# A chunked delta-rule attention with a gated convolution: the dense part taken over pairs of chunks, one merge step over 128 rows, and the order of all instructions written anew

## The chip, the cores and the metric

The kernel runs on one core of a Trainium2 chip. The metric is the device time of one execution in microseconds (us). Engines are named as in the profile: PE multiplies matrices (PEld is its weight load), DVE and ACT are the two vector engines, POOL is the general one, SP issues transfers. All numbers are float32, and the profile counts two matrix instructions for each float32 matmul of the source.

## The reference

Each of 4 x 8 heads has 768 tokens of 48 features. A state of 48 x 48 is updated token by token with the delta rule; the result, heads side by side, goes through a causal convolution of five taps whose sigmoid gates a dense product, and then through a second dense product.

```python
def _attn_ref(q, k, v, beta):
    k_n = k / (norm(k, axis=-1) + 1e-06)
    for t in range(S):
        y[:, :, t] = einsum('bhd,bhde->bhe', q[:, :, t], state)
        v_old = einsum('bhde,bhd->bhe', state, kt)
        state = state + bt[:, :, :, None] * einsum('bhd,bhe->bhde', kt, vt - v_old)

def _moe_ref(x, w_val, conv_w, w_out):      # x: (4, 768, 384)
    for k in range(5):
        gate_pre += conv_w[k] * xp[:, k:k + S, :]
    return (1 / (1 + exp(-gate_pre))) * (x @ w_val) @ w_out
```

## The kernel before, in words

The 768 tokens are cut into 12 chunks of 64 (`C`, `NCH`); two chunks are a pair `g`. In each chunk the 32 heads lie as 16 units in each half of the 128 partitions. Per chunk there are four kinds of work.

**Products of keys and queries.** `kq` multiplies keys with keys and queries on PE; ACT copies the key product to `GL` (`kqevac`), DVE writes the query product times a causal mask (`masked`, called by `att` and `att0`): for head half h = 0 in two operations of 64 rows straight into `R`, for h = 1 in one of 128 rows into `AQ`, which two transfers then bring into `R` (`stack`).

**The triangular inverse.** The state equation needs the inverse of a 64 x 64 triangular matrix per head. Per pair, DVE transposes blocks of `GL` into `TL` (`trans_in`, L463), inverts 16 x 16 blocks there in a long chain of small operations (`coef`, `row`, `mergez8`, `merget8`), and transposes the result out into `XA` and `WB` (`trans_out`, L520). Per chunk, PE and ACT then merge 16 x 16 blocks to 32 (`m16`, `m32`) and 32 to 64 (`lev` twice, with `zevac` and `tevac`), which fills `XX`. In `m16` the weights are `G64` or, in `m32`, `W64`; each matmul uses 64 rows and 64 columns of the array, at four places in turn.

**The recurrence.** `e` (state times keys), `eadd` on DVE, `u` (`XX` times values), `uevac`, `s` (new state into the PSUM tiles `SPS`), `sevac`, and `y` (the chunk's output). `y` needs `Y`, of which one part comes from `US` over a transfer that ACT issues. The chunk's output goes to `X`, 32 of its rows over six transfers of SP from `YSB` (X<-YSB in the rows).

**The dense part**, `moe(ch)`, once per chunk on tiles of 128 features x 256 columns (4 batches x 64 tokens): a scaled copy on ACT (`conv`), twelve multiply-adds on DVE (`tap`, L678), sigmoid on ACT, nine matmuls `val` (L687), three products on DVE (`gate`, L691), six matmuls `outp` (L695), two copies out and four stores.

The order is not a scheduler's: every call is added to a `Plan`, and the tables `ORDER` (numbers of planned calls) and `BANKS` (the PSUM bank for each result) say in which order they are issued. Each engine and each queue takes its own calls in that order. A -1 in `ORDER` is a matmul of zeros (`keep_warm`, L925); there are 31. Loads of chunks 0 to 3 go over SP, later ones over POOL. At the start, the weights, which arrive as 64-bit floats, are turned into float32 by DVE, ACT and POOL (`plan_weights`).

Of the kernel before, what the change touches and what calls it, by code (L numbers as in the profile page):

```python
# [1014 lines left out]
```

## Time and profile before

| | us |
|---|---|
| time, median of 3 runs | 331.96 (329.41 to 334.33) |
| profiled execution, span from first to last instruction | 324.6 |
| PE busy | 280.4 |
| DVE busy | 241.1 |
| ACT busy | 172.1 |
| POOL busy | 77.7 |

The profiled execution's own time is given as its span alone; the median of the runs stands 7.4 above it. Busy times overlap between engines. PE's busy time counts a matmul from its start to its modelled end, so a busy PE may still run at the lower clock: PEclk is the granted TensorE clock as a share of full speed. The mean granted clock of this execution was 0.879.

### The profile page before, as it was taken

What the parts mean: (1) busy time and instruction counts of PE and PEld (TensorE: products, weight loads), DVE (VectorE), ACT (ScalarE), POOL (GpSimd) and SP (SyncE); (2) the same over time, 40 slices, a digit from 0 to 9 for tenths busy, and PEclk for the clock granted to TensorE, in tenths of its full rate; (3) what the DMA queues carried; (4) which work ended last, traced back from release to release, by engine and by line L of the source; (5) the groups of instructions that cost most, each with busy time, mean ns of one, the idle gap of its engine ahead of it and who ended that gap; (6) DMA issues with size and microseconds to landing.
All of it is one profiled execution on the core that took longest, in us unless ns stands there. A gap on an engine that the chain in (4) does not pass through costs nothing.

```text
span 324.6 us, 16708 instructions
## 1 busy us (share of the span) xinstructions
PE 280.4 (86%) x7342; PEld 223.6 (69%) x7342; DVE 241.1 (74%) x602; ACT 172.1 (53%) x454; POOL 77.7 (24%) x156
## 2 busy tenths in 40 slices
...
GB/s 197 217 264 102 256 103 128 82 112 147 131 139 140 177 85 212 61 100 141 137 127 220 30 61 149 193 142 63 34 77 159 95 78 21 6 42 48 79 58 52
DMA packets 50569, 37.84 MB, mean 117 GB/s; under 512 B 37184, under 2 KB 43456, under 8 KB 50496
## 3 DMA queue, kind: packets, MB, share of 16 engines
...
## 4 chain that ended last, share of the span: by engine, by line
PE 49%; DVE 20%; DMA 11%; issue 7%; SPq 4%; ACT 4%; POOL 3%; ACTq 1%; POOLq 0%; DVEq 0%
PE PB L250 24%; PE PB L687 12%; PE PB L695 10%; SPq L237 4%; DMA X<-YSB 4%; DVE GT L678 3%; DMA XX<-in_w_val_dram 3%; DVE KQ L415 2%; PE SPS L250 2%; DMA KQ<-in_qr_dram 2%; DVE PR L489 2%; DMA Y<-US 1%; DVE AQ L415 1%; POOL MASK L276 1%; DVE GL L398 1%
## 5 line engine op out<-in xcount | busy, mean ns | idle before, releaser
L678 DVE SCALAR_TENSOR_TENSOR GT<-X,CW,GT 128x256 f32<-128x256 f32 x144 | 67.9, 497 | 19.4 <-ACT GT L229 17.3
L687 PE MATMUL PB<-X,WV 128*128 128x256 f32 x216 | 59.9, 419 | 2.2 <-issue 2.0
L695 PE MATMUL PB<-WO,GT 128*128 128x384 f32 x144 | 53.3, 511 | 0.7 <-DVE GT L691 0.6
L229 ACT ACTIVATE XX<-PB 32x256 f32<-32x256 f32 (+2 forms) x96 | 39.3, 427 | 19.5 <-PE PB L250 14.1
L687 PEld LDWEIGHTS PB<-X,WV 128*128 128x128 f32 x216 | 41.9, 205 | 10.9 <-issue 3.1
L250 PE MATMUL PB<-KQ 48*64 48x128 f32 (+1 forms) x896 | 36.2, 313 | 15.1 <-DVE QUOT L442 4.0
L250 PEld LDWEIGHTS PB<-KQ 48*64 48x64 f32 x896 | 30.7, 170 | 20.3 <-issue 6.8
L695 PEld LDWEIGHTS PB<-WO,GT 128*128 128x128 f32 x144 | 26.7, 195 | 16.6 <-issue 1.2
L691 DVE TENSOR_TENSOR GT<-PB,GT 128x256 f32<-128x256 f32 x36 | 14.8, 418 | 21.1 <-ACT GT L682 11.4
L250 PE MATMUL PB<-KQ,Y 112*48 112x64 f32 (+2 forms) x768 | 26.5, 227 | 3.3 <-DMA Y<-US 3.3
L229 ACT ACTIVATE GL<-PB 128x256 f32<-128x256 f32 (+1 forms) x44 | 16.3, 403 | 24.7 <-PE PB L250 20.3
L250 PEld LDWEIGHTS PB<-KQ,Y 112*48 112x48 f32 (+2 forms) x768 | 23.8, 128 | 6.4 <-DMA Y<-US 3.8
L582 POOL TENSOR_TENSOR VT<-VT,NRM 128x768 f32<-128x768 f32 x12 | 18.1, 1512 | 40.4 <-DVE NRM L459 19.1
L229 ACT ACTIVATE GT<-X,CW 128x256 f32<-128x256 f32 x36 | 17.8, 504 | 18.3 <-DMA X<-YSB 16.7
L229 ACT ACTIVATE Y<-SPS 48x384 f32<-48x384 f32 (+1 forms) x44 | 20.8, 482 | 7.6 <-PE SPS L250 7.0
L415 DVE TENSOR_TENSOR KQ<-PB,MASK 64x256 f32<-64x256 f32 (+1 forms) x44 | 19.3, 444 | 6.9 <-ACT GT L682 3.1
L250 PE MATMUL PB<-XA,G 64*64 64x16 f32 x768 | 18.0, 222 | 6.7 <-issue 2.9
L250 PEld LDWEIGHTS PB<-XA,G 64*64 64x64 f32 x768 | 16.4, 156 | 9.4 <-issue 3.8
L634 DVE TENSOR_TENSOR VT<-PB,VT 128x384 f32<-128x384 f32 x22 | 11.8, 549 | 12.6 <-PE PB L250 11.7
L250 PE MATMUL PB<-YS,W 64*64 64x32 f32 x768 | 17.5, 237 | 3.5 <-DVE GT L691 1.3
L229 ACT ACTIVATE Y<-PB 64x192 f32<-64x192 f32 x48 | 14.4, 321 | 11.1 <-PE PB L250 7.0
L682 ACT ACTIVATE GT<-GT 128x256 f32<-128x256 f32 x36 | 14.8, 416 | 9.8 <-DVE GT L678 9.5
...
## 6 DMA issues: line engine op xcount, KB each, us to landing
...
```

Of the source, the lines that this page charges most:

```text
L229: A.activation(out=out, in_=in_, func=AF.Copy, **kw)
L237: SP.dma_start(out=dst, in_=src)
L250: PE.matmul(p, lhsT, rhs, start=start, stop=stop, tile_position=(row, col), skip_group_check=True)
L415: V.tensor_tensor(out=AQ[ch % NAQ][:, u:u + n] if v is None else R[ch % NR][r, v, u:u + n], in0=p[r], in1=MASK[h][r].unsqueeze(1).to_broad ...
L489: V.tensor_tensor(out=pr, in0=t8[:, :, 0:i, 0:i], op=ALU.mult, in1=l8[:, :, i, 0:i].unsqueeze(2).to_broadcast([128, 4, i, i]))
L582: G.tensor_tensor(out=v, in0=v, in1=n.unsqueeze(3).to_broadcast([128, 2, HB, D]), op=ALU.mult)
L634: V.tensor_tensor(out=v, in0=bank["e", ch, h][:, 0:HB * D], in1=v, op=ALU.add)
L678: V.scalar_tensor_tensor(out=g, in0=XB[ch % NX][:, m, :, k:k + C], scalar=CW[:, m, k:k + 1], in1=g, op0=ALU.mult, op1=ALU.add)
L682: A.activation(out=g, in_=g, func=AF.Sigmoid, scale=-1.0)
L687: PE.matmul(p[:, 0:B * C], WV[:, k, 128 * m:128 * m + 128], XB[ch % NX][:, k, :, 4:], start=k == 0, stop=k == NKT - 1)
L691: V.tensor_tensor(out=g, in0=bank["val", ch, m][:, 0:B * C].rearrange("p (b t) -> p b t", t=C), in1=g, op=ALU.mult)
L695: PE.matmul(bank["out", ch, i][:, 0:DM], GT[ch % 2][:, k, 2 * i:2 * i + 2, :].rearrange("p b t -> p (b t)"), WO[:, k, :], start=k == 0, st ...
```

## The change

- **Dense part by pairs.** `moe(p, lo, n)` handles 128 tokens of a pair at once: tiles of 128 features x 512 columns. The last two chunks are still done one by one. `X` holds a pair and has two buffers, `GT` five slots.
- **16 to 32 over 128 rows.** `m16` and `m32` contract over all 128 rows: both 64-row halves lie block by block in `XAB` (two copies per pair from `XA`, on POOL, for pair 0 on ACT) and `YS`. There are half as many matmuls, each into one of two column halves of the array, with 32 and 64 columns moved in place of 16 and 32.
- **Masked products.** Both head halves are written to `AQ` by DVE in operations of 128 rows, and four transfers per chunk bring them into `R`, in place of three DVE operations and two transfers.
- **Loads in halves without padding.** Keys, queries and values are loaded by head halves, without the padding rows of before: 48 or 128 rows of 8 units each. The 16 rows of `R` that were padding are filled by POOL at the start (`zR`). `KT`, `VT` and `XX` each have one buffer less.
- `US` goes to `Y` over SP, not ACT. `tevac` is one copy where it was two, and `vscale` is two where it was one. `keep_warm` is called nowhere.
- **Order and banks** are new tables.

```diff
-    NKF, NR, NKTB, NVT, NAQ, NX, NXX, NOS = 4, 4, 3, 3, 2, 3, 4, 3
+    NKF, NR, NKTB, NVT, NAQ, NX, NXX, NOS, NGT = 4, 4, 2, 2, 2, 2, 3, 3, 5
...
-    def masked(p, ch, h, u, n, v):
-
-        r = slice(0, 128) if v is None else slice(64 * v, 64 * v + 64)
-        V.tensor_tensor(out=AQ[ch % NAQ][:, u:u + n] if v is None else R[ch % NR][r, v, u:u + n], in0=p[r],
-                        in1=MASK[h][r].unsqueeze(1).to_broadcast([128 if v is None else 64, n, C]), op=ALU.mult)
+    def masked(p, ch, h, u, n):
+        V.tensor_tensor(out=AQ[ch % NAQ][:, HB * h + u:HB * h + u + n], in0=p, in1=MASK[h].unsqueeze(1).to_broadcast([128, n, C]), op=ALU.mult)
...
+    def xblocks(g, a):
+        r = slice(64 * a, 64 * a + 64)
+        copy(G if g else A, XAB[r, :, 16 * a:16 * a + 16], XA[r])
...
     def l_m16(ch, h):
-        p = bank["m16", ch, h]
-        for pp in range(HB * h, HB * h + HB):
-            for r in (0, 64):
-                to = 64 - r if h else r
-                yield p[to:to + 64, 16 * (pp % HB):16 * (pp % HB) + 16], G64[r:r + 64, unit(ch, pp), :], XA[r:r + 64, unit(ch, pp), :], r, to
+        p = bank["m16", ch]
+        for j in range(HB):
+            x = unit(ch, HB * h + j)
+            yield p[64 * h:64 * h + 64, 32 * j:32 * j + 32], G64[:, x, :], XAB[:, x, :], 0, 64 * h
...
         if what == "U":
-            send(Y[ch % 2][to, v].rearrange("p (h y j) d -> p h y (j d)", h=2, y=2)[:, :, 1], US[ch % 2][other])
-        if what == "A":
-            load(R[ch % NR][to, v, HB:], AQ[ch % NAQ][other])
+            load(Y[ch % 2][to, v].rearrange("p (h y j) d -> p h y (j d)", h=2, y=2)[:, :, 1], US[ch % 2][other])
+        if what != "U":
+            u = slice(HB * what, HB * what + HB)
+            load(R[ch % NR][to, v, u], AQ[ch % NAQ][other if what else to, u])
...
-    def tap(ch, m, k):
-        g = GT[ch % 2][:, m]
-        V.scalar_tensor_tensor(out=g, in0=XB[ch % NX][:, m, :, k:k + C], scalar=CW[:, m, k:k + 1], in1=g, op0=ALU.mult, op1=ALU.add)
...
+    def tap(p, lo, n, m, k):
+        g = gcols(p, m, lo, n)
+        V.scalar_tensor_tensor(out=g, in0=XB[p % NX][:, m, :, lo + k:lo + k + n], scalar=CW[:, m, k:k + 1], in1=g, op0=ALU.mult, op1=ALU.add)
...
+    for i in range(NR):
+        add("POOL", fill, (G, (R[i][32:64, 1], 0.0)), w=[("Rz", i)], kind="zR")
...
     def load_k(ch):
-        fetch(KF[ch % NKF][0:112], kf[ch], ch, [("KF", ch % NKF)], "LKF")
+        for h in range(2):
+            for f in (0, 64):
+                fetch(KF[ch % NKF][f:f + D, HB * h:HB * h + HB], kf[ch, f // 64, :, HB * h:HB * h + HB], ch, [("KF", ch % NKF, h, f)], "LKF")
...
         chain(ch)
-        moe(ch)
+        if ch >= NCH - 2:
+            moe(ch // 2, C * (ch % 2), C)
+        elif ch % 2:
+            moe(ch // 2, 0, 2 * C)
```

Three places of the order follow. The first is DVE at the first inverse (pair 0), from its last reductions to the transposes that end it. Before (PR and TT hold the inverse, TLP is the next pair's input, OS and XX hold raw weights):

```order
L517 TENSOR_REDUCE TT__84<-PR_86 128x2x8x4
L463 STREAM_TRANSPOSE TLP<-GL_73 128x1024
L517 TENSOR_REDUCE TT__84<-PR_85 128x2x8x4
L415 TENSOR_TENSOR KQ<-PB_125,MASK_113 64x512
L520 STREAM_TRANSPOSE WB<-TT__84 128x16x32
L415 TENSOR_TENSOR KQ<-PB_125,MASK_113 64x512
L308 TENSOR_SCALAR XX_79<-XX_79 128x384
L520 STREAM_TRANSPOSE XA<-TT__84 128x16x32
```

And of the change, the same place up to the next pair's input:

```order
L508 TENSOR_REDUCE TT__81<-PR_82 128x2x8x4
L511 STREAM_TRANSPOSE XA<-TT__81 128x16x32
L511 STREAM_TRANSPOSE WB<-TT__81 128x16x32
L405 TENSOR_TENSOR AQ_66<-PB_117,MASK_108 128x256
...
L405 TENSOR_TENSOR AQ_67<-PB_118,MASK_108 128x256
L300 TENSOR_SCALAR OS<-OS 128x384
...
L452 STREAM_TRANSPOSE TLP<-GL_71 128x1024
```

The transpose that opens the second inverse stood ahead of the end of the first; it now stands behind it, behind eight masked products and two sets of weight work.

The second place is POOL ahead of the merge of chunks 8 and 9: W is what `m32` takes as weights, XAB what `m16` moves. Before:

```order
L240 DMA VT_66<-in_vt_dram 128x768
L240 DMA KT_63<-in_kt_dram 128x768
L671 COPY X_92<-X_91 128x12x4
L231 COPY W_75<-WB 32x16x16
L240 DMA KQ<-in_qr_dram 64x1024
L240 DMA KQ<-in_qr_dram 48x1024
L231 COPY W_75<-WB 32x16x16 x3
```

Of the change, ahead of the merge of chunks 6 and 7, the like place:

```order
L232 DMA KQ<-in_kf_dram 48x512
L232 DMA VT_64<-in_vt_dram 128x384
L232 DMA KQ<-in_qr_dram 48x512
L232 DMA KQ<-in_kf_dram 48x512
L232 DMA VT_65<-in_vt_dram 128x384 x2
L226 COPY XAB<-XA 64x32x16
L226 COPY W_73<-WB 32x16x16
L226 COPY XAB<-XA 64x32x16
L226 COPY W_73<-WB 32x16x16 x2
```

Two copies of XA are new, and they and the copies of WB stand behind smaller and more load issues.

The third place is SP in the fourth pair of the change: US is the part of `u` that `y` needs, AQ the masked products, G a block of the next inverse, W as above.

```order
L229 DMA KQ<-AQ_67 64x512
L229 DMA Y_68<-US_78 64x2x192
L229 DMA G_72<-GL_71 16x32x16
L229 DMA Y_68<-US_78 64x2x192
L229 DMA G_72<-GL_71 16x32x16
L229 DMA KQ<-AQ_66 64x512
L229 DMA G_72<-GL_71 16x32x16
L229 DMA X_89<-YSB_91 16x4x64 x2
L229 DMA Y_69<-US_79 64x2x192 x2
```

Before, the rows of US stood in ACT's order, with nothing of SP's ahead of them:

```order
L234 DMA Y_70<-US_81 64x2x192 x2
L234 DMA Y_71<-US_82 64x2x192 x2
```

SP now takes them in turn with transfers that wait for DVE, ACT and PE.

## Rows read from the trace of the kernel before

**Rows 1.** Windows: stretch, length, busy of PE, PEld, DVE, ACT, POOL, granted clock, DMA.
```profile
0.00:71.60 71.60, 50.60 (x1282) 43.11 (x1283) 63.96 (x155) 30.81 (x75) 26.77 (x70) 0.71 0.66 163
71.60:127.20 55.60, 49.27 (x1466) 41.63 (x1459) 40.41 (x107) 33.88 (x91) 19.70 (x35) 0.82 0.61 144
127.20:267.40 140.20, 130.05 (x3530) 101.05 (x3530) 109.64 (x280) 77.95 (x214) 29.36 (x48) 0.94 0.49 112
267.40:305.50 38.10, 36.77 (x1029) 29.05 (x1028) 19.46 (x45) 23.63 (x65) 1.84 (x5) 1.00 0.17 34
305.50:324.60 19.10, 13.72 (x50) 8.79 (x48) 7.65 (x18) 5.81 (x14) 0.00 (x0) 1.00 0.29 62
```
**Rows 2.** Timeline of PE: start, length in us, instructions; in brackets the idle before.
```profile
216.44 1.09 PE L250 MATMUL PB<-KQ,Y 112*48 112x64 f32 x16 [2.69 <-DMA Y<-US]
...
241.30 2.20 PE L695 MATMUL PB<-WO,GT 128*128 128x384 f32 x6
...
244.40 1.10 PE L250 MATMUL PB<-YS,W 64*64 64x32 f32 x64
...
250.72 1.56 PE L687 MATMUL PB<-X,WV 128*128 128x256 f32 x6
...
255.16 1.10 PE L250 MATMUL PB<-KQ,Y 112*48 112x64 f32 x32
```
**Rows 3.** Groups of PE by line, from 71.6 to 127.2: busy us, mean ns, idle before.
```profile
L687 PE MATMUL PB<-X,WV 128*128 128x256 f32 x36 | 11.8, 470 | 1.5 <-issue 1.5
...
L695 PE MATMUL PB<-WO,GT 128*128 128x384 f32 x12 | 4.2, 486 | 0.0
```
**Rows 4.** The same from 127.2 to 267.4.
```profile
L695 PE MATMUL PB<-WO,GT 128*128 128x384 f32 x84 | 32.1, 523 | 0.0
L687 PE MATMUL PB<-X,WV 128*128 128x256 f32 x114 | 32.0, 422 | 0.7 <-issue 0.5
```
**Rows 5.** Groups of DVE by line and shape, whole span, columns as in Rows 3.
```profile
L678 DVE SCALAR_TENSOR_TENSOR GT<-X,CW,GT 128x256 f32<-128x256 f32 x144 | 67.9, 497 | 19.4 <-ACT GT L229 17.3
L415 DVE TENSOR_TENSOR KQ<-PB,MASK 64x256 f32<-64x256 f32 x40 | 16.5, 420 | 6.8 <-ACT GT L682 3.1 <-ACT GL L229 2.5 <-PE PB L250 0.6
...
L691 DVE TENSOR_TENSOR GT<-PB,GT 128x256 f32<-128x256 f32 x36 | 14.8, 418 | 21.1 <-ACT GT L682 11.4 <-PE PB L687 9.2
...
L634 DVE TENSOR_TENSOR VT<-PB,VT 128x384 f32<-128x384 f32 x22 | 11.8, 549 | 12.6 <-PE PB L250 11.7 <-ACT XX L229 0.9
...
L415 DVE TENSOR_TENSOR AQ<-PB,MASK 128x256 f32<-128x256 f32 x20 | 7.8, 417 | 3.0 <-ACT GL L229 2.0 <-PE PB L250 0.9
...
L415 DVE TENSOR_TENSOR KQ<-PB,MASK 64x512 f32<-64x512 f32 x4 | 2.7, 687 | 0.1
```
**Rows 6.** Timeline of DVE at the start, columns as in Rows 2.
```profile
12.24 1.91 DVE L463 STREAM_TRANSPOSE TLP<-GL 128x1024 f32<-128x1024 f32 x1
...
22.72 1.27 DVE L489 TENSOR_TENSOR PR<-TT__84,TLP 128x100 f32<-128x100 f32 x1
...
36.28 1.93 DVE L463 STREAM_TRANSPOSE TLP<-GL 128x1024 f32<-128x1024 f32 x1
...
42.10 1.04 DVE L520 STREAM_TRANSPOSE XA<-TT__84 128x512 f32<-128x512 f32 x1
...
59.58 0.26 DVE L489 TENSOR_TENSOR PR<-TT__84,TLP 128x100 f32<-128x100 f32 x1
...
70.46 1.05 DVE L520 STREAM_TRANSPOSE XA<-TT__84 128x512 f32<-128x512 f32 x1
```
**Rows 7.** Timeline of POOL at the start.
```profile
22.39 1.47 POOL L582 TENSOR_TENSOR VT<-VT,NRM 128x768 f32<-128x768 f32 x1 [11.71 <-DMA VT<-in_vt_dram]
```
**Rows 8.** Groups of POOL by line and shape, columns as in Rows 3.
```profile
L231 POOL COPY W<-WB 32x256 f32<-32x256 f32 x24 | 10.5, 436 | 9.9 <-DVE WB L520 8.9
...
L247 POOL MEMSET XX<- 32x256 f32 x16 | 4.9, 303 | 0.7
```
**Rows 9.** The chain that ended last, at 200 to 240: start, us, what.
```profile
210.89 5.87 DMA X<-YSB
```

More of the change, by code (lines that the diff above doesn't have):

```diff
@@ L199 @@
     XA = one([128, NU, 16], "XA")
+    XAB = one([128, NU, 32], "XAB")
     WB = one([128, NU, 16], "WB")
-    YS = one([128, NU, 32], "YS")
-    XB = tiles(NX, [128, NKT, B, C + 4], "X")
+    YS = one([128, NP, C], "YS")
+    XB = tiles(NX, [128, NKT, B, 2 * C + 4], "X")
     YSB = tiles(2, [112, B, C], "YSB")
-    GT = tiles(2, [128, NKT, B, C], "GT")
-    OS = tiles(NOS, [128, DM], "OS")
+    GTB = one([128, NGT, B, 2 * C], "GT")
+    OSB = one([128, NOS * DM], "OS")
+    OS = [OSB[:, DM * i:DM * i + DM] for i in range(NOS)]
     WV, WO = one([128, NKT, DM], "WV"), one([128, NKT, DM], "WO")
@@ L682, in sig, with val @@
+    def sig(p, lo, n, m):
+        g = gcols(p, m, lo, n)
         A.activation(out=g, in_=g, func=AF.Sigmoid, scale=-1.0)
[L684 to L685 removed]
+    def val(p, lo, n, m):
+        d = bank["val", p, lo, m]
         for k in range(NKT):
[L687 to L691 removed]
@@ L693, in outp, with gate @@
-    def outp(ch, i):
+            PE.matmul(d[:, 0:B * n], WV[:, k, 128 * m:128 * m + 128], XB[p % NX][:, k, :, lo + 4:lo + 4 + n], start=k == 0, stop=k == NKT - 1)
+    def gate(p, lo, n, m):
+        g = gcols(p, m, lo, n)
+        V.tensor_tensor(out=g, in0=bank["val", p, lo, m][:, 0:B * n].rearrange("p (b t) -> p b t", t=n), in1=g, op=ALU.mult)
+    def outp(p, lo, n, i):
         for k in range(NKT):
-            PE.matmul(bank["out", ch, i][:, 0:DM], GT[ch % 2][:, k, 2 * i:2 * i + 2, :].rearrange("p b t -> p (b t)"), WO[:, k, :],
+            g = gcols(p, k, lo, n)
+            PE.matmul(bank["out", p, lo, i][:, 0:DM], g[:, i] if n == 2 * C else g[:, 2 * i:2 * i + 2].rearrange("p b t -> p (b t)"), WO[:, k, :],
@@ L708 @@
             add("ACT", const_eye, (t[:, :, x:x + 16], 0, 16, r), r=["EYE"], w=[n + "z"])
-    add("ACT", const_eye, (YS[:, :, 16:32], 16, 16), r=["EYE"], w=["YSc"])
-    add("ACT", const_eye, (ZS[:, :, 32:64], 0, 32), r=["EYE"], w=["ZSc"])
+    add("POOL", fill, (G, (YS, 0.0), (XAB, 0.0)), w=["YSc", "XABz"], kind="zYS")
+    for h in range(2):
+        r = slice(64 * h, 64 * h + 64)
+        add("ACT", const_eye, (YS[:, :, 32 * h + 16:32 * h + 32], 16, 16, r), r=["EYE"], w=["YSc"])
+    for x in (0, 64):
+        add("ACT", const_eye, (ZS[:, :, x:x + 32], 0, 32), r=["EYE"], w=["ZSc"])
     for h in range(2):
@@ L755, in grams @@
                 toks = [("kp", ch, h) for h in range(2)]
[L756 removed]
+                add("PE", kp, (ch,), r=k_of(ch), w=toks, take=toks)
                 for h in range(2):
@@ L833, in load_v, with tri @@
-    def load_v(ch):
-        fetch(VT[ch % NVT], vt[ch], ch, [("VT", ch % NVT, h) for h in range(2)], "LV")
-        add("POOL", vscale, (ch,), r=[("NRM", ch // 2 % 2)], w=[("VT", ch % NVT, h) for h in range(2)])
+                add("SP" if g and q // 64 == h else "POOL" if g or h else "ACT", wblocks, (g, q, h), r=["WB", "W64z"], w=[("W64", q, h)])
+    def tri(ch):
+        g, c = ch // 2, ch % 2
+        gb = g % 2
+        x = ch % NXX
+        t1, t2 = ("m16", ch), ("m32", ch)
+        add("PE", m16, (ch,), r=[("G64", q) for q in range(0, 128, 32)] + ["G64z"] + [("XAB", a) for a in range(2)], w=[t1], take=[t1])
+        for h in range(2):
+            add("ACT", m16evac, (ch, h), r=[t1, "YSc"], w=[("YS", h)], give=[t1])
+        add("PE", m32, (ch,), r=[("W64", q, h) for q in range(0, 128, 32) for h in range(2)] + ["W64z", "YSc"] + [("YS", h) for h in range(2)],
+            w=[t2], take=[t2])
+        for h in range(2):
+            add("ACT", m32evac, (ch, h), r=[t2, ("XXz", x)], w=[("XX", x, "late", h)] + [("XX", x, h, a) for a in range(2)], give=[t2])
+        t1, t2 = ("lev", ch, 1), ("lev", ch, 2)
+        add("PE", lev, (ch, 1), r=[("GL", gb, h, c, i) for h in range(2) for i in range(2)] + [("XX", x, "late", h) for h in range(2)], w=[t1], take=[t1], kind="lev1")
+        add("ACT", zevac, (ch,), r=[t1], w=["ZS"], give=[t1])
+        add("PE", lev, (ch, 2), r=["ZS", "ZSc"] + [("XX", x, h, a) for h in range(2) for a in range(2)], w=[t2], take=[t2], kind="lev2")
+        for h in range(2):
+            for a in range(2):
+                add("ACT", tevac, (ch, h, a), r=[t2], w=[("XX", x, h, a)], give=[t2])
@@ L844, in chain @@
             toks = [("e", ch, h) for h in range(2)]
-            add("PE", e, (ch,), r=[("KF", ch % NKF)] + [("Y", c2, "S", x, v) for x in range(2) for v in range(2)], w=toks, take=toks)
+            add("PE", e, (ch,), r=k_of(ch) + [("Y", c2, "S", x, v) for x in range(2) for v in range(2)], w=toks, take=toks)
             for h in range(2):
@@ L876, in moe @@
-    def moe(ch):
-        x, g = ch % NX, ch % 2
-        xt = [[("X", x, k)] + [("Xp", x, k, to) for to in (48, 112)] for k in range(NKT)]
-        if ch < NCH - 1:
-            add("POOL", halo, (ch,), r=sum(xt, []), w=[("Xh", (ch + 1) % NX)])
+                add("SP", load, (xcols(ch)[to:to + 16, k], YSB[c2][lo + 16 * k:lo + 16 * k + 16]),
+                    r=[("YSB", c2), ("X", ch // 2 % NX, c2, k)], w=[("Xp", ch // 2 % NX, c2, k, to)], kind="Lx")
+    outs = [0]
+    def moe(p, lo, n):
+        x = p % NX
+        cs = range(2) if n == 2 * C else [lo // C]
+        xt = [[t for c in cs for t in [("X", x, c, k)] + [("Xp", x, c, k, to) for to in (48, 112)]] for k in range(NKT)]
+        xh = [[("Xh", x)] if lo == 0 else [("X", x, 0, k)] + [("Xp", x, 0, k, to) for to in (48, 112)] for k in range(NKT)]
+        gt = [[("GT", gslot(p, m), c) for c in cs] for m in range(NKT)]
+        if p < NG - 1:
+            add("POOL", halo, (p,), r=sum(xt, []), w=[("Xh", (p + 1) % NX)])
+        d = (p, lo, n)
@@ L888, in moe @@
-            add("PE", val, (ch, m), r=sum(xt, []) + [("W", i) for i in range(1, 4)], w=[("val", ch, m)], take=[("val", ch, m)])
-            add("DVE", gate, (ch, m), r=[("val", ch, m)], w=[("GT", g, m)], give=[("val", ch, m)])
-        for i in range(2):
-            o = (2 * ch + i) % NOS
-            add("PE", outp, (ch, i), r=[("GT", g, m) for m in range(NKT)] + [("W", 4 + k) for k in range(NKT)], w=[("out", ch, i)], take=[("out", ch, i)])
-            add("ACT", oevac, (ch, i), r=[("out", ch, i)], w=[("OS", o)], give=[("out", ch, i)])
-            for b in range(2):
-                add("SP", load, (out[2 * i + b, C * ch:C * (ch + 1), :], OS[o][C * b:C * b + C]), r=[("OS", o)], kind="Lo")
+            t = ("val", p, lo, m)
```

213 lines of the change are left out of this document (104 added, 109 removed), and 152 rows, old and new, of the table ORDER.

## The prediction

> **What bounds the kernel now.** I read the windows first, cut where the program's stages change: 71.6 us is the first matmul of the second pair's merge, 127.2 that of the third, 267.4 that of the last, 305.5 the end of the last `y`. Busy time times granted clock tells how much full-speed matmul work a stretch holds [rows 1]. To 71.6, DVE is busy 63.96 us (89%), PE runs at 0.71 of its clock, 1.2 GHz much of the time: DVE sets this stretch. From 71.6 to 127.2 PE holds 49.27 x 0.82 = 40.4 us of full-speed work, 73% of the 55.6 us, and DVE is busy 73%: neither is full, the waits between them and the low clock cost. From 127.2 to 267.4 PE holds 130.05 x 0.94 = 122.2 us, 87% of 140.2, idle only 10.15: PE sets it, with DVE at 78%. From 267.4 to 305.5 PE holds 97%. The last 19.1 us are the last chunk's dense part in a row.
>
> So an edit on PE counts in full from 127.2 on, one on DVE counts to 71.6, and in between either counts in part.
>
> **PE: dense products.** Six matrix instructions of 256 columns take 1.56 us (0.260 each), six of 384 take 2.20 (0.367) [rows 2]: 0.107 per 128 columns more. One of 512 is then 0.474; ends are 0.428 (columns alone) and 0.520 (twice the 256). Five pairs replace 180 by 90: 46.8 against 42.7, so -4.1 us (-8.3 to 0). `outp` keeps its shape and its count.
>
> **PE: 16 to 32.** Sixty-four instructions of 64 rows x 64 columns take 1.10 us, 17 ns each, since four lie in the array side by side [rows 2]. Nearest to the new shape is `y`: 112 rows, only two column halves, 64 columns moved, 32 instructions in 1.10 us, 34 ns each [rows 2]. A chunk's `m32` becomes 32 such: 1.10 us, the same as before; so I cost this edit at nothing. Ends: 17 ns would save 0.55 in each of 24 groups, 13.2 us; 64 weight columns against `y`'s 48, a third more, would add 8.9.
>
> **DVE.** A tap now takes 67.9 / 144 = 0.472 us; the masked products go from 420 to 687 ns when columns go from 256 to 512 [rows 5], so 0.267 for 256 more, and a wide tap is 0.739 (0.472 to 0.944, no gain). Sixty wide and 24 narrow ones: 55.7, so -12.2. Gates: 14.8 becomes 15 x 0.678 + 6 x 0.411 = 12.6, -2.2. Masked products: 40 of 64 x 256 (16.5), 20 of 128 x 256 (7.8) and six of 512 columns (4.1) become 40 and four of 128 rows: 15.6 + 2.7, so -10.1 [rows 5]. Together -24.5 of DVE's 241. ACT loses work as well (wide copies, 24 issues); with 53% it bounds no stretch, so I count nothing.
>
> **To 71.6.** Ahead of the second XA (70.46 [rows 6]) the masked products fall from 10.0 us (eight of 0.420, six of 0.687, six of 0.417) to 6.9 (four of 0.687, ten of 0.417), and two sums of 0.549 move in front [rows 5]: -2.0. Against it stand two waits. POOL first fills `R`, `YS` and `XAB`, six fills of 1024 columns, at most 4 x 0.303 each [rows 8], 7.3 us; the masks come behind, and DVE needs the first mask amid the corrections that end before 12.24 [rows 6]. DVE has some 3 us of its own fills there; I take +2 (0 to 7.3). And the transpose that opens the second inverse, at 36.28 before and so ahead of the first XA at 42.10 [rows 6], now comes behind it, with `kq` of chunk 3 behind `m16` on PE and four transfers in front. DVE has eight masked products and two sets of weight work to cover that; beyond it I take +4 (0 to 6.9, its lead before). Sum for this stretch +4 (-2 to +12): the first inverse ends earlier, the second later.
>
> **71.6 to 127.2.** Before, 36 `val` and 12 `outp` instructions lie here [rows 3]: 9.4 + 4.4 us. By the new order it is all of pair 0: 18 wide ones (8.5) and 24 `outp` (8.8). Work becomes 40.4 + 3.5 = 43.9. DVE has about 5 us less here. As the first two chunks' state no longer has to be caught up with, I take the use of the next stretch, and one point more for a freer DVE: 88%, 49.9 us, -5.7.
>
> **127.2 to 267.4.** Of 114 `val` and 84 `outp` [rows 4], 29.6 + 30.8 us, remain 54 wide and 66: 25.6 + 24.2. Work becomes 111.6, at 88% 126.8 us: -13.4. DVE falls from 109.6 by some 14, to three quarters of the shorter stretch, so it does not take over.
>
> **The end.** Twelve wide taps (8.9 us) now stand ahead of the last chunk's `eadd` on DVE, and work behind `eadd` is the state's; PE has pair 4 as cover: +1 (0 to 5). After the last `y`, one more group of `outp` (2.20) than before is left: +1.
>
> **POOL and DVE.** A product on DVE at 22.72 took 1.27 us, its like at 59.58 0.26 [rows 6]; from 22.39 to 23.86 POOL ran a product of its own [rows 7], and DVE's ended 0.13 us behind it. Ten copies `XAB` of 512 columns, 0.436 to 0.872 each by the copies of 256 [rows 8], are new on POOL, 4.4 to 8.7 us. They come when DVE has taps: I take +1 (0 to 8.7). The Trainium skill, "SBUF — State Buffer", section "Who interferes with whom", says that a DVE instruction with two SBUF inputs blocks, for a whole instruction, against one of POOL that reads SBUF; these rows agree, and by that rule all 8.7 us could fall on the taps, which have two such inputs: 328 in place of 320.
>
> **SP and the loads.** SP's order gains 56 issues by the program's text (+24 masked products, +24 US, +28 loads of the first chunks, -20 stores). Steady pairs hold 40 in place of 36; I count nothing while `y` stands behind the next chunk's `e`; the cost without that cover is rival three. Smaller loads on POOL are hidden by two chunks of lead.
>
> **Sum.** +4 - 5.7 - 13.4 + 1 + 1 + 1 = -12.1 against a span of 324.6: 312.5. The median of the runs, 331.96, stands 7.4 above this span; I carry that over: **320 us**.
>
> **Rivals.**
>
> *One: instructions, not columns, are what small matmuls cost.* Then `m16` and `m32` halve. For it: 17 ns each whether 16 or 32 columns move. Against: `y` with 34 ns. Twenty of the 24 groups lie where PE binds: 20 x 0.55 = 11 less, 309. The Trainium skill, "TensorEngine Tiling (Array Packing)", section "Instruction Overhead", puts about 60 cycles on each matmul, however few its columns, which speaks for this rival; this trace's 17 ns are below 60 cycles at 2.4 GHz, so the rows do not bear the figure out.
>
> *Two: no change.* The stretch to 127.2 stays at its 73%, since the second inverse comes late and POOL's copies, behind load issues, hold `m16`: 43.9 / 0.73 = 60.1, +4.5. With +4 ahead, the next stretch at its old 87% (128.3, -11.9) and +3 for the rest, -0.4: 332. For it: most of what is saved is DVE's, and PE's own saving is 4 us. Against: DVE binds the start.
>
> *Three: slower.* US goes over SP, behind issues that wait for DVE and PE, in order. When it is late, `y` is, then `X` (a wait of 5.87 us for X<-YSB stands in the chain [rows 9]), then taps and the sums behind them. One such wait of PE is there now: 2.69 us [rows 2]. Once in each of 11 chunks: 29.6, so 350. It makes the kernel over 2% slower from 7 chunks on ((338.6 - 320) / 2.69). Against: the order puts `e`, `u` or dense work between.
>
> **Chances.** My forecast 52%, own range 310 to 328; rival one 15% (302 to 312); two 20% (328 to 336); three 13% (over 338). The range leaves out rival three and the lowest third of rival one: 304 to 335. Two per cent, 325.3 and 338.6, is about what can be told from no change here (three runs spread from 329.41 to 334.33). Of my forecast, 7 points lie above 325.3. Faster by over 2%: 45 + 15 = 60%; within: 7 + 20 = 27%; slower: 13%.
>
> **What would show it.** In the changed profile: wide `val` at 0.47 us each, `m32` still near 1.1 us per group at full clock, DVE's busy time near 217, wide taps near 0.74. `m16` of chunk 2 near 75, of chunk 4 near 125, the last `y` ending near 291. PE's use from the third pair's merge on at 88% or more. Waits of PE for Y<-US of over 2 us in most chunks would mean rival three; `m16` waiting for `XAB` or DVE in each pair, rival two. The prediction is wrong at its root if the gaps that the new order closes are larger than the two DVE-bound stretches let me count, or if new waits open in the recurrence.

## The result and the profile after

The changed kernel takes 316.15 us (median; 311.61 to 317.48), the kernel before on the same chip 330.69: a ratio of 0.9567 (95% interval 0.9455 to 0.9678), so it is faster. The profiled execution took 315.52 us, with a span of 313.8. Run again on chip 11, the changed kernel lay at 311.92 to 317.81 and the kernel before in two groups, two runs near 320 and nine at 325 to 332; the ratio there is 0.9804 (0.9716 to 0.9893), since ratios are taken from undisturbed runs alone, and of the kernel before those are the two near 320. The gain is real in both; the ratios put it at 4.3% and 2.0%, the second on two runs of the kernel before alone.

The windows of the changed kernel, cut at the same places as [rows 1] (first matmul of the second, third and last pair's merge, end of the last `y`), with the same columns:

```profile
0.00:75.60 75.60, 42.99 (x1225) 37.20 (x1226) 58.91 (x150) 35.72 (x84) 34.51 (x86) 0.66 0.62 154
75.60:124.70 49.10, 40.88 (x1130) 29.57 (x1130) 36.62 (x82) 28.97 (x68) 24.60 (x40) 1.00 0.56 134
124.70:250.50 125.80, 117.11 (x3066) 85.56 (x3066) 94.09 (x223) 72.08 (x177) 50.30 (x94) 0.95 0.51 126
250.50:293.60 43.10, 41.95 (x945) 31.10 (x945) 17.97 (x31) 25.28 (x62) 5.74 (x11) 0.87 0.35 87
293.60:313.80 20.20, 15.82 (x60) 11.13 (x60) 7.91 (x18) 6.48 (x15) 0.00 (x0) 0.99 0.26 73
```

Against [rows 1] the stretches changed by +4.0, -6.5, -14.4, +5.0 and +1.1 us, in sum -10.8. The fourth, the last merge and what follows it, is the one that is far from the forecast. In the third, PE's dense groups, which answer to [rows 4]:

```profile
L688 PE MATMUL PB<-X,WV 128*128 128x512 f32 x54 | 24.8, 603 | 0.0
L697 PE MATMUL PB<-WO,GT 128*128 128x384 f32 x66 | 23.7, 500 | 0.0
```

DVE's groups by line and shape, which answer to [rows 5] (busy us, mean ns, idle before):

```profile
L679 DVE SCALAR_TENSOR_TENSOR GT<-X,CW,GT 128x512 f32<-128x512 f32 x60 | 42.9, 757 | 11.2 <-ACT GT L224 10.7
L405 DVE TENSOR_TENSOR AQ<-PB,MASK 128x256 f32<-128x256 f32 x40 | 15.9, 418 | 31.7 <-ACT GL L224 15.7 <-ACT GT L224 9.6 <-PE PB L242 4.9
...
L623 DVE TENSOR_TENSOR VT<-PB,VT 128x384 f32<-128x384 f32 x22 | 11.5, 547 | 22.2 <-PE PB L242 22.2
L679 DVE SCALAR_TENSOR_TENSOR GT<-X,CW,GT 128x256 f32<-128x256 f32 x24 | 11.1, 483 | 4.3 <-ACT GT L224 3.7
L692 DVE TENSOR_TENSOR GT<-PB,GT 128x512 f32<-128x512 f32 x15 | 10.2, 685 | 1.0 <-ACT Y L224 0.5 <-PE PB L688 0.4
```

Sixty wide taps keep DVE busy for 42.9 us, 0.715 each; all 40 narrower masked products are of one shape now. DVE's total is 215.5 us.

DVE at the start, which answers to [rows 6] (start, length, what; in brackets the idle before):

```profile
13.97 1.96 DVE L452 STREAM_TRANSPOSE TLP<-GL 128x1024 f32<-128x1024 f32 x1
...
32.77 1.05 DVE L511 STREAM_TRANSPOSE XA<-TT__81 128x512 f32<-128x512 f32 x1
...
41.56 1.31 DVE L405 TENSOR_TENSOR AQ<-PB,MASK 128x256 f32<-128x256 f32 x3 [5.63 <-ACT GL L224]
45.60 0.36 DVE L300 TENSOR_SCALAR OS<-OS 128x384 f32<-128x384 f32 x1 [2.73 <-ACT OS L298]
...
51.21 1.97 DVE L452 STREAM_TRANSPOSE TLP<-GL 128x1024 f32<-128x1024 f32 x1
...
73.16 1.05 DVE L511 STREAM_TRANSPOSE XA<-TT__81 128x512 f32<-128x512 f32 x1
```

POOL between the last of these and the merge at 75.60:

```profile
74.27 1.27 POOL L226 COPY XAB<-XA 64x512 f32<-64x512 f32 x2 [3.90 <-DVE XA L511]
```

The first inverse ends 9.3 us earlier than before, the second opens 14.9 later and ends 2.7 later. Between them DVE stands idle for 8.4 us. PE's waits, summed over the span (total, times, longest), begin with the reason:

```profile
PE PB L242 <- DMA KQ<-in_kf_dram: 14.2, 1, 14.2
PE PB L242 <- issue: 6.9, 6, 2.3
PE PB L242 <- POOL XAB L226: 3.7, 4, 1.7
PE SPS L242 <- ACT Y L224: 3.6, 2, 2.1
```

PE waited 14.2 us for the keys of chunk 2, whose loads stood in SP's order behind many small ones and behind transfers that wait for DVE. The waits for Y<-US of [rows 2] have all but gone, those for XAB are new.

### The profile page after: what moved, and what is told of

It reads as the page before. It is cut to its first block, busy times and chain, and to the rows that moved or that the text cites. A ratio compares the mean times of both kernels' runs of the same rounds, so it can differ in the third digit from the quotient of the medians.

```text
span 313.8 us, 14806 instructions
## 1 busy us (share of the span) xinstructions
PE 258.8 (82%) x6422; PEld 194.6 (62%) x6422; DVE 215.5 (69%) x504; ACT 168.5 (54%) x404; POOL 115.2 (37%) x230
## 4 chain that ended last, share of the span: by engine, by line
PE 48%; DVE 4%; ACT 3%; DMA 3%; issue 2%; SPq 2%; POOL 2%; ACTq 0%; POOLq 0%; DVEq 0%
PE PB L242 23%; PE PB L688 13%; PE PB L697 10%; SPq L229 2%; DMA X<-YSB 2%; DMA Y<-US 2%; PE SPS L242 1%; ACT Y L224 1%; DVE PR L490 1%; POOL XAB L226 1%; ACT OS L224 1%; DVE PR L502 1%; DVE VT L623 1%; ACT X L224 0%; DVE TT__81 L483 0%
## 5 line engine op out<-in xcount | busy, mean ns | idle before, releaser
L679 DVE SCALAR_TENSOR_TENSOR GT<-X,CW,GT 128x512 f32<-128x512 f32 (+1 forms) x84 | 54.0, 678 | 15.5 <-ACT GT L224 14.4
L242 PE MATMUL PB<-KQ 48*64 48x128 f32 (+1 forms) x896 | 35.7, 310 | 18.9 <-DMA KQ<-in_kf_dram 14.2
L688 PE MATMUL PB<-X,WV 128*128 128x512 f32 (+1 forms) x126 | 49.7, 541 | 1.7 <-DMA X<-YSB 1.7
L224 ACT ACTIVATE XX<-PB 32x512 f32<-32x512 f32 (+1 forms) x72 | 36.9, 518 | 22.3 <-PE PB L242 21.5
L405 DVE TENSOR_TENSOR AQ<-PB,MASK 128x256 f32<-128x256 f32 (+1 forms) x44 | 18.5, 442 | 31.7 <-ACT GL L224 15.7
L688 PEld LDWEIGHTS PB<-X,WV 128*128 128x128 f32 x126 | 22.9, 190 | 19.9 <-issue 15.5
L571 POOL TENSOR_TENSOR VT<-VT,NRM 128x384 f32<-128x384 f32 x24 | 20.6, 859 | 26.9 <-DMA VT<-in_vt_dram 14.0
L224 ACT ACTIVATE Y<-SPS 64x384 f32<-64x384 f32 (+1 forms) x44 | 20.4, 482 | 16.9 <-PE SPS L242 16.6
L242 PE MATMUL PB<-YS,W 128*64 128x64 f32 x384 | 18.0, 258 | 5.5 <-issue 2.1
L242 PE MATMUL PB<-XAB,G 128*64 128x32 f32 x384 | 16.8, 249 | 4.2 <-POOL XAB L226 3.7
L232 POOL DMA_DIRECT2D KQ<-in_kf_dram x32 | 16.8, 527 | 8.8 <-PE PB L242 8.6
```

Source lines behind the costliest of these rows:

```text
L224: A.activation(out=out, in_=in_, func=AF.Copy, **kw)
L232: G.dma_start(out=dst, in_=src)
L242: PE.matmul(p, lhsT, rhs, start=start, stop=stop, tile_position=(row, col), skip_group_check=True)
L405: V.tensor_tensor(out=AQ[ch % NAQ][:, HB * h + u:HB * h + u + n], in0=p, in1=MASK[h].unsqueeze(1).to_broadcast([128, n, C]), op=ALU.mult)
L571: G.tensor_tensor(out=v, in0=v, in1=n.unsqueeze(2).to_broadcast([128, HB, D]), op=ALU.mult)
L679: V.scalar_tensor_tensor(out=g, in0=XB[p % NX][:, m, :, lo + k:lo + k + n], scalar=CW[:, m, k:k + 1], in1=g, op0=ALU.mult, op1=ALU.add)
```

## The experiments

The runs come from three chips, each with runs of the kernel before beside it, whose medians stand in the table. These move between 322.43 and 327.66, and by 1.9 us on the same chip, so a difference of some 2 us between two medians can't be told from none, least of all across chips. Lines of code are shifted by a few in some variants.

| run | chip | median us (range) | kernel before, median us | ratio to the kernel before |
|---|---|---|---|---|
| after_again | 11 | 314.53 (311.92 to 317.81) | 327.66 | 0.9804 (0.9716 to 0.9893) |
| val_halves | 10 | 313.93 (312.83 to 314.47) | 324.34 | 0.9707 (0.9666 to 0.9747) |
| tap_halves | 10 | 316.54 (313.05 to 321.09) | 324.34 | 0.9747 (0.9676 to 0.9818) |
| mask_halves | 10 | 321.11 (315.34 to 326.78) | 324.34 | 0.9832 (0.9772 to 0.9892) |
| all_halves | 11 | 321.99 (320.44 to 323.45) | 327.66 | 1.0052 (0.9990 to 1.0113) |
| warm_end | 10 | 313.95 (310.95 to 317.50) | 324.34 | 0.9670 (0.9609 to 0.9731) |
| start | 11 | 323.81 (316.25 to 326.13) | 327.66 | 0.9927 (0.9688 to 1.0166) |
| best1 | 11 | 329.75 (329.32 to 333.61) | 327.66 | 1.0320 (1.0225 to 1.0415) |
| start2 | 10 | 314.10 (311.69 to 321.63) | 322.43 | 0.9747 (0.9692 to 0.9802) |
| xab2 | 10 | 313.79 (310.30 to 320.82) | 322.43 | 0.9712 (0.9640 to 0.9784) |
| warm_xab | 3 | 312.37 (309.51 to 315.93) | 324.17 | 0.9628 (0.9558 to 0.9698) |
| before_no_warm | 10 | 332.02 (328.39 to 334.80) | 322.43 | 1.0297 (1.0222 to 1.0373) |

### Shapes: which of the wider operations count

**The change run again** (after_again). 

> The changed kernel as it is, for comparison with the others on the same chip. Both theories: 0.955 to 0.975 of the time before.

0.9804 came, above what was expected. Variants below that can't be told from the changed kernel (val_halves, warm_end, start2, xab2) have ratios of 0.967 to 0.975 on chip 10.

**Wide val undone** (val_halves).

```diff
-        for k in range(NKT):
-            PE.matmul(d[:, 0:B * n], WV[...], XB[p % NX][:, k, :, lo + 4:lo + 4 + n], ...)
+        for b in range(0, B, 2):
+            for k in range(NKT):
+                PE.matmul(d[:, b * n:b * n + 2 * n], WV[...], XB[p % NX][:, k, b:b + 2, lo + 4:lo + 4 + n], ...)
```

> The changed kernel, with each 512-column val product issued as two of 256 columns (90 matrix instructions of 0.474 us become 180 of 0.260): 4.2 us more work on PE, nothing else moved. Theory (PE sets the time from the second pair's merge on): the time rises by the full price, 3.5 to 4.5 us, to about 320. Rival (PE has slack, what counts is DVE's relief and the order): no change, under 1 us.

No change: 313.93 against 314.53 (and 313.95 of warm_end, beside it on its chip). But the price itself was wrong, so this says nothing yet on PE's slack. The timeline of PE in the changed kernel:

```profile
136.31 1.15 PE L242 MATMUL PB<-YS,W 128*64 128x64 f32 x32 [0.67 <-ACT YS L224]
137.39 1.10 PE L242 MATMUL PB<-ZS,XX 32*32 32x64 f32 x64
138.42 2.84 PE L688 MATMUL PB<-X,WV 128*128 128x512 f32 x6
141.19 0.75 PE L242 MATMUL PB<-XX,GL 32*32 32x32 f32 x64
142.95 5.42 PE L688 MATMUL PB<-X,WV 128*128 128x512 f32 x12
148.30 1.10 PE L242 MATMUL PB<-ZS,XX 32*32 32x64 f32 x64
```

and with halves:

```profile
138.63 2.86 PE L692 MATMUL PB<-X,WV 128*128 128x256 f32 x12
141.42 0.75 PE L242 MATMUL PB<-XX,GL 32*32 32x32 f32 x64
143.51 5.45 PE L692 MATMUL PB<-X,WV 128*128 128x256 f32 x24
148.89 1.10 PE L242 MATMUL PB<-ZS,XX 32*32 32x64 f32 x64
```

From start to next start, six of 512 columns take 2.77 us and twelve of 256 take 2.79; a doubled run adds 2.58 and 2.59, so 0.215 us per 256 columns in either shape. The length of a group also holds a part that comes once per run of one kind: twelve in the kernel before took 2.86, as here, where two groups of six [rows 2] have 3.12. Twice the instructions cost nothing, one longer run in place of two saves some 0.2 us. The Trainium skill, "TensorEngine Tiling (Array Packing)", section "Instruction Overhead", has some 60 cycles for each matmul whatever its columns. As a cost added to each matmul this trace does not show it: six more instructions took 0.02 us more. Whether it holds as a least time for matmuls of few columns, 256 columns can't show, and neither can the forecast's 17 ns, which are the distance of two starts with four instructions in the array side by side.

**Wide taps undone** (tap_halves).

```diff
-            V.scalar_tensor_tensor(out=g, in0=x, scalar=CW[:, m, k:k + 1], in1=g, ...)
+        for b in range(0, B, 2):
+            V.scalar_tensor_tensor(out=g[:, b:b + 2], in0=x[:, b:b + 2], scalar=CW[:, m, k:k + 1], in1=g[:, b:b + 2], ...)
```

> The changed kernel, with each of the 60 wide taps on DVE issued as two of 256 columns: 60 x (0.944 - 0.71) = 14 us more on DVE, all behind the second pair's merge. Theory (behind that point PE binds and DVE has room): 0 to 3 us more, the 3 from the twelve taps of pair 4 that stand ahead of the last chunk's sum. Rival (the gain comes from DVE being freed): 10 us or more, most of the gain of the change lost.

DVE's group of taps in that run:

```profile
L682 DVE SCALAR_TENSOR_TENSOR GT<-X,CW,GT 128x256 f32<-128x256 f32 x144 | 63.1, 500 | 11.9 <-ACT GT L224 11.3
```

144 taps took 63.1 us where 84 took 54.0: 9.1 more, not 14. The time rose by 2.0 us in the median (2.6 against val_halves on the same chip), no more than can be told; the rival's 10 is excluded.

**Masked products of head half 0 undone** (mask_halves).

```diff
-        V.tensor_tensor(out=AQ[ch % NAQ][:, ...], in0=p, in1=MASK[h]..., op=ALU.mult)
+        for r in ([slice(0, 128)] if h else [slice(0, 64), slice(64, 128)]):
+            V.tensor_tensor(out=AQ[ch % NAQ][r, ...], in0=p[r], in1=MASK[h][r]..., op=ALU.mult)
```

> The changed kernel, with the masked products of head half 0 cut into two operations of 64 rows, as they were before the change: two more of 512 columns (0.69 us each) and twenty more of 256 (0.42), 9.8 us more on DVE, of which about 3.1 to 3.5 us stand ahead of the second inverse's transpose out (at 73.16 us). Theory (DVE sets the start and nothing behind it): the second transpose out 2 to 3 us later and the time up by as much; less, if the 8.4 us in which DVE stands idle between 35.9 and 45.6 take it in. Rival (DVE counts everywhere): 8 to 10 us more.

```profile
74.62 1.04 DVE L513 STREAM_TRANSPOSE XA<-TT__81 128x512 f32<-128x512 f32 x1
```

Between the two: 6.6 us more than after_again in the median, but on another chip; against val_halves, beside it on the same chip, the ratio is 0.0125 higher, some 4 us. So 4 to 7 us, on 8 to 10 us more of DVE (225.8 against 217.5 and 215.5 in the two profiles of the changed kernel). The second transpose out moved by 1.5 us only, to 74.62, so most of it is not paid at the start, against the theory. The profiled execution (span 317.9) doesn't show one place: it is 1.4 us longer than the changed kernel's first in the first stretch, 1.5 in the second, 1.7 in the fourth.

**All three undone** (all_halves): the edits above together. 

> The changed kernel's order, pairs and banks with the instruction shapes of before in the dense part and the masked products: val in 256 columns, taps in 256, head half 0 of the masked products in 64 rows: 24 us more on DVE, no more columns on PE. Theory (the gain comes from the order and from long runs of one kind on PE; shapes count only where DVE binds, to the second transpose out, and in the taps ahead of the last sum): 4 to 7 us above the changed kernel, so 7 to 11 us of the gain remain. Rival (wider shapes make the gain): all of it lost, 12 us or more above.

7.5 us above the changed kernel on the same chip (321.99 against 314.53), so just above the theory's range; the rival's 12 us did not come. How much of the gain remains can't be said: by the medians 5.7 us (321.99 against 327.66), by the ratio, which stands on the two runs near 320, nothing. Of the single edits the one on the masked products costs most; those on the dense part's wide forms can't be told from none. By the ratios of chip 10, tap_halves and mask_halves stand 1 and 4 us above val_halves, in sum less than the 7.5 of all three together. Why the three together lose more isn't explained; the third stretch of this profile is 128.93 us long, where tap_halves has 125.66 and mask_halves 125.13.

### The start

**Keys first** (start): a new order of the first 60 us. SP's order, the chunk in words:

```diff
-  ... QR of 0 to 3, KT, KF and QR of 2 and 3 between AQ transfers, weights, realign ...
+  ... QR of 0 and 1, KF and QR of 2, QR and KF of 3, G, AQ, VT, AQ, realign, KT, AQ, weights ...
```

> The changed kernel with the order of the start written anew and nothing else: the keys and queries of chunks 2 and 3 are loaded right behind those of chunks 0 and 1, ahead of the transfers that wait for DVE's masked products; chunk 4's loads on POOL come later; the key products of chunks 2 and 3 and their copies stand ahead of the first merge, the masked products of chunk 2 inside the first inverse, and the second inverse opens right behind the first. Theory (DVE sets the start, and the 8.4 us that it stands idle between 35.9 and 45.6 us, behind PE's wait of 14.2 us for chunk 2's keys, are a loss that the forecast put at 4): the transpose in of the second inverse moves from 51.2 to near 37 us, the second transpose out and the second pair's merge come 6 to 8 us earlier (near 68 us), the time falls by 5 to 8 us. Rival (the recurrence of chunks 0 and 1 on PE and ACT sets the start as well): DVE's idle time only moves to its wait for the sums of chunk 1, gain under 3 us.

The transpose in came at 39.08 us, but the merge at 80.83, 5 us later, and the time went up, by 9 us in the median (runs from 316.25 to 326.13) and by 4 by the ratio, whose interval is wide. DVE and the merge in that run:

```profile
39.08 1.95 DVE L455 STREAM_TRANSPOSE TLP<-GL 128x1024 f32<-128x1024 f32 x1 [2.74 <-DMA GL<-GL]
50.05 0.36 DVE L303 TENSOR_SCALAR OS<-OS 128x384 f32<-128x384 f32 x1 [9.02 <-ACT OS L301]
...
80.83 1.92 PE L245 MATMUL PB<-XAB,G 128*64 128x32 f32 x32 [0.80 <-POOL XAB L229]
```

The weights now stood behind AQ, VT and KT on SP; DVE waited 9.02 us for them and ACT, in its own order, 5.24. A wait was moved, not removed.

**Keys first, mended** (start2).

```diff
+        sp = ch < NSP and not (ch == 3 and kind in ("LKF", "LQR"))
-        add(*(("SP", load) if ch < NSP else ("POOL", bulk)), ...)
+        add(*(("SP", load) if sp else ("POOL", bulk)), ...)
```

> The start once more, with the faults of the first try taken out: the keys and queries of chunk 3 go over POOL beside SP, chunk 4's loads come in POOL ahead of the first merge's copies, and the first large weight is fetched before the masked products' transfers, so that DVE doesn't wait for it behind the second inverse's transpose in. Theory (DVE sets the start, once nothing that it needs is queued behind other issues): transpose in of the second inverse near 36 us, no idle time of DVE over 3 us up to the second transpose out, second pair's merge near 68 us (75.6 before this edit), 5 to 8 us off the time, to 307 to 311. Rival (the recurrence of the first two chunks sets the start as well): merge at 73 or later, under 3 us.

DVE's waits in that run, to 76 us:

```profile
DVE AQ L409 <- DMA KQ<-AQ: 5.0, 2, 3.7
...
DVE X L304 <- ACT X L302: 3.2, 1, 3.2
DVE OS L304 <- ACT OS L302: 1.9, 1, 1.9
```

DVE's transposes there, and the merge on PE:

```profile
41.75 1.91 DVE L456 STREAM_TRANSPOSE TLP<-GL 128x1024 f32<-128x1024 f32 x1
...
73.22 1.05 DVE L515 STREAM_TRANSPOSE XA<-TT__81 128x512 f32<-128x512 f32 x1
...
75.66 1.36 PE L246 MATMUL PB<-XAB,G 128*64 128x32 f32 x32
```

The transpose in is at 41.75 (51.21 in the changed kernel), the second transpose out at 73.22 (73.16), the merge at 75.66. DVE waits 10.1 us in sum, no less than the 8.4 in the changed kernel, in other places: for `AQ` to be carried off, then for weights. The theory's 5 to 8 us did not come. Whether the recurrence of the first chunks would have held the merge there anyway isn't settled by it, since DVE's waits stayed.

### Clock, XAB and the zeros

**Zeros around the end's waits** (warm_end): `keep_warm` seven times behind `u` of chunk 9, three times behind its `s`.

```diff
-    ..., 1371, ..., 1380, 1302, ...
+    ..., 1371, -1 (seven times), ..., 1380, -1 (three times), 1302, ...
```

> The changed kernel with ten matmuls of zeros put back into PE's order: seven behind u of chunk 9, where PE stood idle for 1.55 us, three behind its s, where it waited 0.48 us for XAB. Theory (the last merge and the work around it ran at a granted clock of 0.50 from about 248 to 262 because PE fell idle just ahead of it, and that is the 4 us by which the end came out above the forecast): the granted clock stays at 1.00 there, the stretch from the last merge to the last y falls from 43.1 to about 38 us, the time by 4 to 5 us, to about 311.5. Rival (the clock falls whatever PE does, or the late XAB is what costs): no change, within 1 us; if the zeros stand in the way of s, 1 us more.

The stretch from the last merge to the end of the last `y`, in the changed kernel's first profile:

```profile
250.48:293.57 43.09, 41.94 (x945) 31.09 (x945) 17.97 (x31) 25.30 (x62) 5.76 (x11) 0.86 0.35 87
```

with the zeros:

```profile
253.15:294.96 41.81, 38.60 (x946) 27.15 (x945) 17.97 (x31) 25.62 (x62) 5.78 (x11) 1.00 0.35 89
```

and in the changed kernel run again, without them:

```profile
254.02:295.84 41.82, 38.09 (x945) 26.86 (x945) 17.89 (x31) 24.54 (x60) 5.78 (x11) 1.00 0.34 90
```

At a granted clock of 1.00 the stretch takes 41.8 us, with or without zeros; the lower clock costs 1.3. The other 3.7 of the 5.0 that the end lost are not the clock: at 1.00, PE is busy for 38.1 us of the 41.8 and idle for 3.7, where in the kernel before it was busy for 36.8 of 38.1 [rows 1].

**XAB at once, with loads moved behind it** (best1): start and warm_end, and

```diff
-            add("POOL" if g else "ACT", xblocks, (g, a), ...)
+            add("ACT" if g == 0 or g in (2, 3, 5) and a == 1 else "POOL", xblocks, (g, a), ...)
```

with POOL's copy ahead of its load issues. 

> The start of the run above, the ten matmuls of zeros around u and s of chunk 9, and one of the two XAB copies of pairs 2, 3 and 5 on ACT beside the other on POOL, with the transpose into XA ahead of that into WB in pair 2 and the copies ahead of load issues. Theory (m16 waits for XAB for 0.5 to 1.7 us a pair because DVE's last transpose and two copies in a row stand ahead of it): 2 us less from the copies, 1 to 4 from the clock of the end, on top of the start: 7 to 12 us below the changed kernel. Rival (a wait that is shortened is found again at the next one, since the latencies of ACT and the transfers behind the merge remain): no better than the start alone, within 1.5 us.

15 us slower than the changed kernel on the same chip, 6 slower than the start alone. POOL in that run:

```profile
223.91 0.22 POOL L671 COPY X<-X 128x48 f32<-128x48 f32 x1
254.91 0.60 POOL L229 COPY XAB<-XA 64x512 f32<-64x512 f32 x1 [30.78 <-DVE XA L514]
255.46 0.21 POOL L671 COPY X<-X 128x48 f32<-128x48 f32 x1
255.70 0.60 POOL L235 DMA_DIRECT2D VT<-in_vt_dram  x1
256.30 0.54 POOL L235 DMA_DIRECT2D KT<-in_kt_dram  x1
```

and PE's longest wait there (total, times, longest):

```profile
PE SPS L245 <- DMA KT<-in_kt_dram: 8.2, 2, 4.7
```

POOL waited 30.78 us for `XA` with the load of `KT` queued behind it, and `s` then waited for `KT`.

**XAB on two engines, no load moved** (xab2): the same edit, with the loads left in front. 

> The changed kernel with one of the two XAB copies of pairs 2, 3 and 5 on ACT, beside the other on POOL, and pair 2's transpose into XA ahead of that into WB; no load is moved behind a copy this time. Theory (each shortened wait of PE for XAB counts once): m16 waits for XAB under 0.5 us in these pairs, where it waited 1.69, 0.58 and 0.48 us: 1 to 2 us off the time. Rival (the wait is found again behind the merge): nothing, within 1 us.

PE's waits for XAB fall from 3.7 us in sum to 0.4. The median is 0.7 us lower than the changed kernel's, on another chip: not to be told from no change.

**Zeros in PE's waits** (warm_xab): xab2, and `keep_warm` 36 times ahead of chunk 2's `kq`, six times each at three other waits. 

> The XAB copies as in xab2, and matmuls of zeros put into PE's waits: 36 into the 14.2 us ahead of chunk 2's key products, six each ahead of the first merge's last step (a wait of 2.4 us there), ahead of s of chunk 1 (2.1) and ahead of s of chunk 9 (1.6). Theory from the kernel before without its keep_warm, which came out 3% slower (what PE does in its waits sets the granted clock of the work behind): the clock stays at 1.00 from 31 us on, where it was 0.50 to 0.8 up to 64, the 20 us of matmuls there take up to 8 us less, the second pair's merge comes 3 to 6 us earlier than the 74 us of xab2, and the time falls to 307 to 311. Rival (DVE and the latencies of ACT and the transfers set the start, PE's clock there is off the path): merge of the second pair within 1.5 us of 74, time within 2 us of xab2.

The zeros filled 9.9 us, then PE was idle for 4.52 us more, and `kq` ran at the low level all the same:

```profile
16.39 9.91 PE L971 MATMUL SPS<-ZW 128*128 128x128 f32 x72
30.82 3.81 PE L247 MATMUL PB<-KQ 48*64 48x128 f32 x64 [4.52 <-DMA KQ<-in_kf_dram]
```

The merge came at 75.62, as the rival had it: so the start's clock was not raised where it was wanted, and the theory was not tried as meant. 312.37 us is the lowest median of all, 2.2 us under the changed kernel and 1.4 under xab2, but on a chip of its own; its ratio's interval overlaps with that of xab2, so no gain is shown. The granted clock did rise over the whole execution, to 0.925 in the mean of the six runs against 0.885 in xab2, without a gain that can be told.

**The kernel before without keep_warm** (before_no_warm): the 31 entries -1 taken out of `ORDER`. 

> The kernel before the change with its 31 calls of keep_warm left out, nothing else. Theory (20 of them fill a wait of PE at 30.8 us in which DVE sets the time; the others stand in waits): no change, within 1% either way. Rival (their 12.8 us of PE's time cost, and a part of the change's gain is that they are gone): 3 to 6 us faster. Second rival (they hold the clock up for the work behind them): 2 to 4 us slower.

3% slower, more than any theory had. The sign is the second rival's, and so is the clock over all runs: the six runs without zeros have a mean granted clock of 0.843 to 0.880, 0.857 on average, the eleven of the kernel before beside them 0.873 to 0.931, 0.893 on average. The profile is of the run with the highest clock of the six; its stretches carry 0.69, 0.85, 0.94, 1.00 and 0.99, against 0.71, 0.82, 0.94, 1.00 and 1.00 in [rows 1], and don't show where the 9.6 us come from. That the zeros earn them through the clock fits, and is not shown: warm_xab raised the mean clock as much and gained no such time.

## Why the prediction was right, step by step

- **The sum and the case.** 312.5 was forecast for the span, 313.8 came; 320 for the time, 316.15 came. It is the forecast's own case. The 7.4 us carried from span to time were mostly chance: of the changed kernel's executions each took 1.7 us more than its span, and its median stands 2.4 above the profiled span, so in the kernel before a faster execution than the median had been profiled. Span against span the gain is 10.8, median against median 14.5. Rival one falls: `m32` takes 1.15 us with 32 instructions, 1.10 with 64 [rows 2]. The forecast's 17 ns were no evidence on the cost of one instruction: with four in the array side by side they are the distance of two starts. Rival three falls: PE hardly waits for Y<-US. Rival two's sign, a wait for XAB, is there in four pairs of five, 3.7 us in sum, but the stretch that it was to hold back took 49.1 us, not 60.1.
- **To the second merge, +4.** +4.0 came, by luck. The first inverse opened 1.7 us later (13.97 against 12.24), near the +2 taken for fills and masks, and ended 9.3 earlier, not 2.0; the second opened 14.9 later, ran faster and ended 2.7 later. The other 1.3 are the two copies into `XAB`, which now stand between the transpose out and the merge and had no term here. Nor did the late opening alone set the end: in start2 the second inverse opened 9.5 us earlier and, with other waits behind that, ended at the same time. "SP gains 56 issues, I count nothing" failed as a description: PE's 14.2 us for chunk 2's keys come from there. What it costs isn't shown: start2 fetched them sooner, and the merge did not move.
- **To the third, -5.7, and to the last, -13.4.** -6.5 and -14.4. The second of these is right in its mechanism: the dense groups are the 54 and 66 of the forecast, PE holds 117.11 x 0.95 = 111.3 us of full-speed work (111.6 forecast), 88% of the stretch as forecast, and run again the stretch took 125.83 us. The first hit with luck: PE held 40.88 x 1.00 = 40.9 us of work, not 43.9, at 83%, not 88%, and the errors cancel. That is the work of before (40.4), done at a clock of 1.00 in place of 0.82: PE was busy for 8.4 us less and idle for 1.9 more. Run again, at 0.93, the stretch took 52.34 us; what raised the clock there stays open.
- **Dense products, -4.1.** Mis-sized in its cause: 0.474 against 0.260 per instruction was read from the lengths of groups, which hold a part that comes once. Undoing the wide form costs nothing. What is saved is one start per run: at most 15 x (2 x 1.49 - 2.77) = 3.2 us, from six of 256 columns in 1.49 and six of 512 in 2.77, start to next start.
- **16 to 32, nothing.** As forecast: `m16` and `m32` keep their time with half the instructions.
- **DVE, -24.5 to 217.** 215.5 came; wide taps 0.715 against 0.739. What it is worth was split wrongly: only the masked products ahead of the second transpose were to count. By mask_halves, the 128-row form is worth 4 to 7 us in all, of which the 1.5 us at the second transpose are the start's share; by tap_halves the wide taps 1 to 3, which can't be told from none; by val_halves wide `val` none.
- **POOL and DVE, +1.** Not seen by itself. The ten `XAB` copies took 6.1 us, in the middle of the 4.4 to 8.7 taken; the sixty wide taps took 42.9 in all, less than the 44.3 forecast, so the 8.7 that could have fallen on them did not.
- **The end, +1.** Failed: +5.0. "PE has pair 4 as cover" was wrong: the merge of the last two chunks runs from 250.48, pair 4's first `val` at 269.37, since it needs `y` of chunk 9 and its transfers:

```profile
250.48 3.63 PE L242 MATMUL PB<-XAB,G 128*64 128x32 f32 x64 [0.48 <-POOL XAB L226]
...
269.37 2.81 PE L688 MATMUL PB<-X,WV 128*128 128x512 f32 x6 [0.60 <-DMA X<-YSB]
```

In the kernel before, a `val` group stood 2 us behind the start of that merge, and more followed:

```profile
267.39 2.10 PE L250 MATMUL PB<-XA,G 64*64 64x16 f32 x128
269.42 1.56 PE L687 MATMUL PB<-X,WV 128*128 128x256 f32 x6
```

In between PE now has little but one chunk's recurrence and the merge. Of the five us 1.3 are the clock, and at full clock the other 3.7 are 2.4 more of PE idle and 1.3 more of PE busy. The last +1 came as +1.1.

- **What had no term.** `keep_warm` goes, and the sum did not price it. In the kernel before it was worth 3%, about as much as the whole gain. If prices add, which no run here shows, the rest of the change (order, pairs, loads) makes up for it; the new order was never tried by itself, so its share stays open. In the changed kernel, zeros put back at ten places (warm_end) or 54 (warm_xab) gained nothing that can be told. The sum took the term at nothing without a reason; as far as it goes, being right was luck.
